# Two more warming matmuls, half as many idle matmuls and another written-out order in a fused attention and mixer kernel

## The chip, the core and the metric

The kernel runs on one core of a Trainium2 chip. The metric is device time in microseconds (us), the median of several executions; lower is better. One further execution was taken with the hardware profiler, and its page and trace are what the prediction reads.

A core has five engines that run their own instruction queues in order: TensorE (PE in the profile; its weight loads stand apart as PEld), VectorE (DVE), ScalarE (ACT), GpSimd (POOL) and SyncE (SP). In this kernel POOL issues the loads, SP issues the stores and the transposing transfers, and PE does every product.

## The reference

For 8 batches, 12 heads, 448 positions and a head width of 64:

```python
scores = scale * np.matmul(q, k.transpose(0, 1, 3, 2))
attn = np.maximum(scores, 0.0) ** 2 / S
x = np.matmul(attn, v)          # then heads side by side: x is (8, 448, 768)
xt = x.transpose(0, 2, 1)
h = np.maximum(xt @ w_tok1, 0.0) @ w_tok2      # 448 -> 256 -> 448 over positions
u = x + h.transpose(0, 2, 1)
h2 = np.maximum(u @ w_ch1, 0.0) @ w_ch2        # 768 -> 1536 -> 768 over channels
return u + h2
```

There is no softmax: scores are clipped at zero, squared and multiplied with v. Inputs and output are float32; products are made in bfloat16.

## The kernel before

The attention is cut into 24 sessions of four heads, three sessions to a batch. The 448 positions are seven chunks (c = 0 to 6) of 64. The channel mixer works by batches and 128-channel blocks, and for its second product by pairs of 128-row tiles, 14 pairs in all. For the last two batches the first channel product, and for all pairs the second one, is made by a scheme of seven block products instead of eight (names Q and P), with sums and differences made on VectorE.

Nothing is scheduled by a planner at run time or at build time. Every operation has a name, and one long string, `ORDER`, lists the names in the order in which they are issued. An entry is `name:how`. For PE operations `how` gives the PSUM banks (0 to 7) that the operation writes; for evictions, copies and sums it is A or D, the engine (ACT or DVE) that does it. Because each engine's queue is filled in this order, `ORDER` decides the sequence on each engine, and the semaphores that follow from the data decide who waits. The check in `run` is only that each name stands behind what it depends on:

```python
            o = self.ops[name]
            assert name not in done and all((d.name in done for d in o.deps)), name
```

The names, with the lines that the profile shows:

- `ldk`, `ldq`, `ldv` s.half: loads of session s on POOL (L286); `ldf`: the first q, loaded in float32 on SP (L345) and turned to bfloat16 by `cast` (L270 on ACT, L272 on DVE); `wt1`, `wt2`, `wc1`, `wc2`: loads of weights (L297, L304, L312, L321). `ident` makes the unit matrix on POOL (masks.py:199).
- `Ts`: transposes of k and q of session s on PE (L391), 56 matmuls of 64 rows, for session 0 in two halves of 28; `cp`: their copy out of PSUM (L270, L272). From session 12 on the transposes are made by transfers (`xk`, `xq`, on SP, after the copies `ik`, `iq`).
- `Ss.c`: scores, four 64-row matmuls (L432) into two banks; `rs.c.e`: eviction of one bank with the clip at zero (L264 on ACT, L266 on DVE); `qs.c`: the square, always on DVE (L439).
- `Vs.c`: the product with v, four 64-row matmuls (L456), which needs the square `qs.c`; `xe`: its eviction (L466 on ACT, L468 on DVE).
- `X`: transposes of x on PE (L491) for the first eight sessions, in halves of four matmuls for the first three, else eight at once; `xc`: their copy into `x_sb`; later sessions use the transfer `xd` on SP.
- `t1` (L500), eviction `rt`, `t2` (L509), sum `u` (L513): the position mixer; `ub`: transfers of its result into `u_sb` on SP.
- `C1.b.e`: first channel product, six matmuls (L545), eviction `c1e` (L264, L266); `Q` (L617) with `m`, `y`, `n`, `h`, `g`: the same for the last two batches.
- `P` (L710) with `s1` to `s4` (L697) and the adds `a`, `b`, `c`, `f` (L725, L727): second channel product; `ws`: the weight sums that it needs; `st`: stores (L759).
- `fill:bank*n`: n idle matmuls on zeros into a bank (L806). They compute nothing that is used; they keep PE busy.

Operations T, S and V use 64 of the array's 128 rows for one matmul and run several side by side; all others use 128 rows. The prediction calls a change from one to the other a change of grouping.

Ahead of `ORDER` PE gets warming matmuls on zeros (L335), 512 columns each. The loads reuse their buffers in rings (four each for k and q, three for v), and a load stands in POOL's queue until the session that held its buffer has been used.

Of the kernel before, what the change touches and what calls it, by code (L numbers as in the profile page):

```python
# [61 lines left out]
ldf.1 ldk0.1 ldf.0 ldk0.0 ldk1.1 ldq1.0 ldq1.1 ldk1.0 cast1.0:A cast1.1:D ldv0.0 ident cast0.0:D cast0.1:A ldv0.1  # L62
T0.1:0 T0.0:1 ldk2.0 cp0.1:A cp0.0:D ldq2.0 fill:2*13 S0.6:23 ldk2.1 S0.2:45 S0.0:67 r0.6.0:A r0.6.1:D S0.1:10
ldq2.1 r0.2.0:A r0.2.1:D S0.4:23 r0.0.0:A ldk3.0 r0.0.1:D S0.3:45 r0.1.1:A ldv1.1 r0.1.0:D S0.5:67 r0.3.1:A ldv1.0
q0.0:D r0.5.1:A fill:0*4 T1.0:01 r0.5.0:A r0.3.0:D ldk3.1 cp1.1:A cp1.0:D ldq3.1 q0.1:D r0.4.1:A ldq3.0 fill:5*19
S1.4:57 S1.1:64 q0.2:D r0.4.0:A S1.2:01 ldq5.0 r1.1.0:A r1.1.1:D fill:3*3 S1.0:32 wt1.1 r1.2.0:A q0.3:D V0.0:64
r1.2.1:A wt1.0 r1.0.1:D V0.1 r1.0.0:A V0.2 q0.4:D T2.0:01 r1.4.1:A ldv2.0 q0.5:D r1.4.0:A S1.3:23 V0.3 ldv2.1
cp2.1:A cp2.0:D ldk5.1 q1.0:D r1.3.1:A fill:7*15 S2.0:75 wt2 q0.6:D S1.6:01 r1.3.0:A r1.6.1:A q1.1:D ldq4.0 S1.5:32
V0.4 r1.6.0:A q1.2:D V0.5 ldk4.1 r1.5.0:A r1.5.1:D V0.6 r2.0.1:A S2.2:10 r2.0.0:D ldk4.0 xe0.1:A q1.3:D xe0.0:A
ldq4.1 r2.2.0:A q1.4:D fill:3*21 X0.0:3 r2.2.1:A q1.5:D S2.3:25 ldv3.1 V1.0:74 xc0.0:A q1.6:D V1.1 ldk6.1 r2.3.0:A  # L70
V1.2 q2.0:D S2.1:61 r2.3.1:A ldq5.1 X0.1:0 q2.2:D r2.1.0:A V1.3 S2.4:32 r2.1.1:A xc0.1:D V1.4 ldv3.0 T3.0:56 q2.3:D
r2.4.0:A V1.5 r2.4.1:A q2.1:D V1.6 cp3.1:A cp3.0:D t1.0.1:0 ldv4.0 xe1.1:D xe1.0:A ldk5.0 fill:1*5 S3.2:13 q2.4:D
rt0.1:A S3.0:25 V2.0:64 ldv4.1 r3.2.1:A r3.0.1:D V2.1 r3.0.0:A S2.5:70 wc1.1 r3.2.0:D S2.6:35 r2.5.0:A V2.2 r2.5.1:D
r2.6.1:A V2.3 ldq6.0 S3.5:21 q3.0:D r2.6.0:A V2.4 S3.3:70 ldq6.1 r3.5.1:A q2.5:D r3.5.0:A q2.6:D fill:5*11 V2.5
r3.3.1:A S3.1:53 q3.2:D X1.0:1 r3.3.0:A t2.0.1:2 q3.5:D r3.1.1:A t1.0.0:0 r3.1.0:A xc1.0:D V2.6 q3.3:D T4.0:73
rt0.0:A ldv5.0 xe2.1:A q3.1:D cp4.1:A ldk6.0 cp4.0:D fill:1*7 X2.1:1 X1.1:5 ldk7.0 t2.0.0:0 u0.1:D xe2.0:A t1.1.0:4
ldv5.1 xc1.1:A xc2.1:D S4.0:73 u0.0:D rt1.0:A S3.4:62 wc1.0 r4.0.1:A t1.1.1:1 r4.0.0:D r3.4.0:A V3.0:54 r3.4.1:D
S3.6:03 rt1.1:A V3.1 r3.6.1:A S4.4:76 r3.6.0:D V3.2 S4.3:12 r4.4.1:A q3.4:D V3.3 r4.3.1:A X2.0:3 r4.3.0:D S4.6:06
r4.4.0:A V3.4 xc2.0:D t2.1.0:2 r4.6.1:A q3.6:D S4.5:17 r4.6.0:A V3.5 ldk8.1 q4.0:D S4.2:36 r4.5.1:A V3.6 u1.0:D
t1.2.0:0 r4.5.0:A ldv6.0 t2.1.1:7 r4.2.1:A r4.2.0:D wc2.11 t1.2.1:1 rt2.0:A xe3.1:D xe3.0:A S4.1:26 T5.0:30 u1.1:D  # L80
ldq7.1 rt2.1:A r4.1.1:A r4.1.0:D X3.0:4 ldq7.0 cp5.1:A t2.2.1:5 cp5.0:D ldk7.1 t2.2.0:1 xc3.0:A q4.1:D V4.0:76
# [5 lines left out]
ldq8.1 S6.1:76 r6.0.0:A r6.0.1:D V5.5 S6.4:03 r6.1.1:A V5.6 ldq8.0 r6.1.0:D r6.4.0:A C1.0.0a:1 xe5.0:D wc2.12
xe5.1:A X4.0:4 q6.0:D r6.4.1:A X5.0:6 ldv7.1 q6.1:D xc4.0:A t2.3.0:7 xc5.0:D C1.0.2a:0 u3.0:D t1.5.0:2 q6.4:D q6.5:D
t1.4.0:5 rt5.0:A C1.0.0 rt4.0:A C1.0.1a:3 c1e0.0:D C1.0.2 t2.5.0:4 c1e0.2:A C1.0.1 u5.0:D S6.6:67 c1e0.1:A T7.0:25
r6.6.0:D r6.6.1:A S6.2:10 S6.3:43 ldk11.0 cp7.0:D cp7.1:A t2.4.1:6 r6.3.1:D ldv8.0 t2.5.1:7 r6.3.0:A t2.4.0:2 u4.1:D  # L90
ldq9.1 r6.2.0:A C1.0.4:5 u4.0:D r6.2.1:A ldk10.1 u5.1:D ldk10.0 S7.3:34 q6.2:D c1e0.4:A S7.0:61 ldv8.1 V6.0:20
r7.0.1:A q6.3:D C1.1.2:7 ldq9.0 r7.0.0:A q6.6:D r7.3.0:A ldq10.1 r7.3.1:D V6.1 c1e1.2:A S7.4:51 wc2.21 q7.0:D
T8.0:63 r7.4.1:A r7.4.0:D V6.2 S7.1:47 wc2.22 cp8.1:A C1.1.5:1 cp8.0:D ldq10.0 r7.1.1:A r7.1.0:D q7.3:D ldq12.0 V6.3
c1e1.5:A S8.0:56 S7.2:37 q7.1:D ldk11.1 V6.4 r7.2.0:A C1.1.7:4 r7.2.1:D ldk12.1 r8.0.1:A r8.0.0:D C1.1.1:1 q7.2:D
c1e1.7:A q7.4:D q8.0:D V7.0:37 c1e1.1:A V6.5 S8.1:65 ws1.1:D V7.1 V6.6 r8.1.1:A V7.2 r8.1.0:D S7.6:41 xe6.1:A
C1.0.5:5 ws1.0:D xe6.0:A r7.6.1:A r7.6.0:D ub0.0 S8.3:60 q8.1:D c1e0.5:A S7.5:21 C1.1.0:4 r8.3.1:A r7.5.0:D ub0.1
# [105 lines left out]
def kernel(ctx: ExitStack, tc: tile.TileContext, q: bass.AP, k: bass.AP, v: bass.AP, moe_w_tok1: bass.AP, moe_w_tok2: bass.AP, moe_w_ch1: bass.AP, moe_w_ch2: bass.AP, out: bass.AP):  # L202
    nc = tc.nc
    B, H, S, D = q.shape
# [129 lines left out]
    for i in range(9):  # L334
        nc.tensor.matmul(warm_ps, lhsT=warm[:, :128], rhs=warm, start=True, stop=True)  # L335
# [451 lines left out]
    for (s, a), o in ue.items():  # L787
        b, i = divmod(s, GS)
# [48 lines left out]
```

## Time and profile before

| what | value |
|---|---|
| median of 3 runs | 353.52 us (352.86 to 354.24) |
| time of the profiled execution | 354.84 us |
| span from its first to its last instruction | 353.1 us |
| mean granted TensorE clock | 0.997 |
| matmuls in the trace | 3645 |
| of these warming / idle matmuls | 9 / 98 |
| DMA | 48.74 MB, mean 138 GB/s |

How to read the lines that follow. On the page, part 1 gives each engine's busy time, its share of the span and its instructions; part 4 gives the chain of work that ended last, by engine. A row of stretches gives the stretch and its length and then, for PE, PEld, DVE, ACT and POOL, the busy time and in parentheses the number of instructions; then the clock, the share of the DMA engines and GB/s. A row of the timeline gives start, length, engine, line, operation, output and input with shapes, and the number of like instructions merged; in square brackets stands the idle time of the engine before it and what ended it. Instructions on one engine overlap in the pipeline, so the price of one among its like is the distance of starts, not its length. A row of DMA issues ends with size and median time from issue to landing.

### The profile page before, as it was taken

What the parts mean: (1) busy time and instruction counts of PE and PEld (TensorE: products, weight loads), DVE (VectorE), ACT (ScalarE), POOL (GpSimd) and SP (SyncE); (2) the same over time, 40 slices, a digit from 0 to 9 for tenths busy, and PEclk for the clock granted to TensorE, in tenths of its full rate; (3) what the DMA queues carried; (4) which work ended last, traced back from release to release, by engine and by line L of the source; (5) the groups of instructions that cost most, each with busy time, mean ns of one, the idle gap of its engine ahead of it and who ended that gap; (6) DMA issues with size and microseconds to landing.
All of it is one profiled execution on the core that took longest, in us unless ns stands there. A gap on an engine that the chain in (4) does not pass through costs nothing.

```text
span 353.1 us, 9074 instructions
## 1 busy us (share of the span) xinstructions
PE 345.2 (98%) x3645; PEld 193.3 (55%) x3645; DVE 304.3 (86%) x581; ACT 215.9 (61%) x443; POOL 92.4 (26%) x157
## 2 busy tenths in 40 slices
PE   7999999999999999999999999999999999999994
PEld 4666556545556555556545565554555565555662
DVE  2799998899988998967699899998989987878973
ACT  3899987888936579874298617778746601452000
POOL 8866515630624523226201602040200000000000
PEclk9999999999999999999999999999999999999998
DMA  8999999799898989999959996779794523730346
GB/s 156 159 173 145 201 190 147 99 183 123 105 193 158 170 147 219 172 162 149 171 111 171 164 167 95 120 124 161 146 110 93 132 44 66 168 65 0 77 115 168
DMA packets 93434, 48.74 MB, mean 138 GB/s; under 512 B 65808, under 2 KB 90064, under 8 KB 93392
## 3 DMA queue, kind: packets, MB, share of 16 engines
q0 software_dynamic: 25904, 21.47, 43.7%
q1 hardware_dynamic: 67168, 26.30, 42.0%
q8 instruction: 28, 0.46, 0.6%
q10 hardware_dynamic: 320, 0.39, 0.4%
q14 instruction: 14, 0.11, 0.1%
HBM read 43.38 MB, written 11.01 MB: 154 GB/s over the span
## 4 chain that ended last, share of the span: by engine, by line
PE 93%; DVE 3%; POOL 1%; issue 1%; ACT 1%; POOLq 0%
PE m_ps L710 27%; PE m_ps L545 24%; PE sc_ps L432 10%; PE acc_ps L456 9%; PE m_ps L617 7%; PE t_ps L500 6%; PE h_ps L509 5%; DVE sq L439 2%; PE kqT_ps L391 2%; PE x_ps L491 1%; PE fill_ps L806 1%; POOL kq_raw L286 1%; ACT sq L264 0%; DVE sq L266 0%; DVE kqT L272 0%
## 5 line engine op out<-in xcount | busy, mean ns | idle before, releaser
L264 ACT ACTIVATE sq<-sc_ps 128x448 bf16<-128x448 f32 x225 | 108.2, 568 | 20.1 <-PE sc_ps L432 19.6
L439 DVE TENSOR_TENSOR sq<-sq 128x896 bf16<-128x896 bf16 x168 | 97.1, 617 | 0.3
L545 PE MATMUL m_ps<-uT_sb,wc 128*128 128x448 bf16 x432 | 90.5, 353 | 0.0
L266 DVE TENSOR_SCALAR sq<-sc_ps 128x448 bf16<-128x448 f32 x111 | 65.2, 618 | 13.3 <-PE sc_ps L432 12.8
L264 ACT ACTIVATE r_sb<-m_ps 128x448 bf16<-128x448 f32 (+3 forms) x93 | 40.1, 464 | 39.5 <-PE m_ps L545 38.0
L545 PEld LDWEIGHTS <-wc 128*128 128x128 bf16 x432 | 40.0, 98 | 42.5 <-issue 8.1
L432 PE MATMUL sc_ps<-kqT 64*64 64x448 bf16 x672 | 57.7, 364 | 0.5
L286 POOL DMA_DIRECT2D v_raw<-in_v_dram x48 | 29.4, 621 | 106.8 <-PE acc_ps L456 68.9
L456 PE MATMUL acc_ps<-sq,v_raw 64*64 64x448 bf16 x672 | 55.1, 354 | 0.0
L710 PEld LDWEIGHTS <-r_sb 128*128 128x128 bf16 x336 | 32.2, 98 | 23.2 <-issue 2.5
L725 DVE TENSOR_TENSOR out_sb<-m_ps,u_sb 128x384 f32<-128x384 f32 x56 | 31.0, 553 | 9.7 <-PE m_ps L710 9.6
L286 POOL DMA_DIRECT2D kq_raw<-in_q_dram x46 | 28.9, 639 | 31.5 <-PE acc_ps L456 16.0
L286 POOL DMA_DIRECT2D kq_raw<-in_k_dram x48 | 29.9, 635 | 24.0 <-PE kqT_ps L391 15.2
L710 PEld LDWEIGHTS <-sums 128*128 128x128 bf16 x252 | 24.4, 98 | 17.6 <-issue 0.7
L513 DVE TENSOR_TENSOR uT_sb<-h_ps,xT 128x448 bf16<-128x448 f32 x48 | 29.1, 618 | 4.7 <-PE h_ps L509 4.6
L432 PEld LDWEIGHTS <-kqT 64*64 64x64 bf16 x672 | 22.8, 107 | 18.0 <-issue 9.7
L710 PE MATMUL m_ps<-wc_t,r_sb 128*128 128x384 bf16 x168 | 31.4, 326 | 0.0
L710 PE MATMUL m_ps<-wc,r_sb 128*128 128x384 bf16 x168 | 31.3, 326 | 0.0
L710 PE MATMUL m_ps<-wc_t,sums 128*128 128x384 bf16 x168 | 30.4, 326 | 0.0
L456 PEld LDWEIGHTS <-v_raw 64*64 64x64 bf16 x672 | 20.6, 106 | 16.5 <-issue 9.9
L264 ACT ACTIVATE r_sb<-t_ps 128x512 bf16<-128x512 f32 (+1 forms) x26 | 14.8, 567 | 23.6 <-PE t_ps L500 23.4
L727 DVE TENSOR_TENSOR out_sb<-m_ps,out_sb 128x384 f32<-128x384 f32 x42 | 22.9, 554 | 4.1 <-PE m_ps L710 3.6
(65 smaller groups left out, 345.3 us busy)
## 6 DMA issues: line engine op xcount, KB each, us to landing
out_dram<-out_sb SPq DMA_DIRECT2D x52, 192.0 KB, 3.0
kq_raw<-in_k_dram POOLq DMA_DIRECT2D x48, 112.0 KB, 4.5
v_raw<-in_v_dram POOLq DMA_DIRECT2D x48, 112.0 KB, 5.0
kq_raw<-in_q_dram POOLq DMA_DIRECT2D x46, 112.0 KB, 4.9
wc<-in_moe_w_ch_dram POOLq DMA_DIRECT2D x2, 1152.0 KB, 11.6
wc<-in_moe_w_ch_dram POOLq DMA_DIRECT2D x3, 576.0 KB, 10.7
u_sb<-uT_sb SPq DMA_TRANSPOSE x54, 3.5
sums<-in_moe_w_ch_dram POOLq DMA_DIRECT2D x1, 576.0 KB, 9.1
```

The lines of the kernel that those rows point to most:

```text
L264: nc.scalar.activation(out, ps, AF.Relu)
L266: nc.vector.tensor_scalar(out=out, in0=ps, scalar1=0.0, scalar2=None, op0=ALU.max)
L286: nc.gpsimd.dma_start(out=raws[t][s % NR[t]][64 * half:64 * (half + 1)], in_=src[b, h0:h0 + 2].rearrange('e (p c) d -> p e (c d)', c=KC))
L432: nc.tensor.matmul(o.ps[e][64 * half:64 * (half + 1), :S], lhsT=lhsT, rhs=rhs, start=True, stop=True, skip_group_check=True)
L439: sq_ops[s, c] = [add(Op(f'q{s}.{c}', 'DVE', lambda o: nc.vector.tensor_tensor(out=buf, in0=buf, in1=buf, op=ALU.mult), ev))]
L456: nc.tensor.matmul(o.ps[half][64 * e:64 * (e + 1), :S], lhsT=r[rows, e, c * D:(c + 1) * D], rhs=sq[rows, e, :], start=c == 0, stop=c == KC ...
L513: nc.vector.tensor_tensor(out=uTs[bb % 2][:, 2 * i + a, off:off + S].rearrange('n (c p) -> n c p', c=KC), in0=t2.ps[:, :S].rearrange('n (p ...
L545: nc.tensor.matmul(ps[:, :S], lhsT=wc1[:, g, e * 128:(e + 1) * 128], rhs=uT[:, g, off:off + S], start=g == 0, stop=g == CC - 1)
L617: nc.tensor.matmul(banks[into][:, :S], lhsT=lhs[:, g, k * 128:(k + 1) * 128], rhs=rhs[:, g], start=after is None and g == 0, stop=g == GH ...
L710: nc.tensor.matmul(banks[into][:, :HN], lhsT=lhs[:, e], rhs=wc2[w][:, e], start=after is None and e == 0, stop=e == EH - 1, skip_group_che ...
L725: nc.vector.tensor_tensor(out=out_[:, cols].rearrange('n (g d) -> n g d', d=128), in0=banks[into][:, :HN].rearrange('n (g d) -> n g d', d= ...
L727: nc.vector.tensor_tensor(out=out_[:, cols], in0=banks[into][:, :HN], in1=out_[:, cols], op=ALU.add)
```

## The change

The diff has two parts. The first adds two warming matmuls:

```diff
-    for i in range(9):
+    for i in range(11):
         nc.tensor.matmul(warm_ps, lhsT=warm[:, :128], rhs=warm, start=True, stop=True)
```

The second replaces the whole string `ORDER`. It holds the same 1,946 operations; the entries `fill` go from nine (13, 4, 19, 3, 15, 21, 5, 11, 7: 98 idle matmuls) to six (7, 4, 19, 3, 12, 4: 49). Its first lines:

```diff
-ldf.1 ldk0.1 ldf.0 ldk0.0 ldk1.1 ldq1.0 ldq1.1 ldk1.0 cast1.0:A cast1.1:D ldv0.0 ident cast0.0:D cast0.1:A ldv0.1
-T0.1:0 T0.0:1 ldk2.0 cp0.1:A cp0.0:D ldq2.0 fill:2*13 S0.6:23 ldk2.1 S0.2:45 S0.0:67 r0.6.0:A r0.6.1:D S0.1:10
+ldf.1 ldk0.1 ldf.0 ldk0.0 ldk1.1 ldq1.0 cast1.0:A cast1.1:D ldk1.0 ldq1.1 ident cast0.0:A cast0.1:D ldv0.0 T0.1:0
+ldv0.1 T0.0:1 cp0.1:A ldk2.0 cp0.0:D ldq2.1 fill:2*7 S0.0:23 S0.5:45 S0.4:67 ldq2.0 r0.0.0:A r0.0.1:D S0.2:01
...
```

Between the two orders the sequence of all engines differs, and so do banks and, for some evictions, the engine: 419 entries on ACT and 575 on DVE become 420 and 574. The loads have another sequence on POOL (`ldv0.0` now behind `ident`; of the weights of the second channel product, `wc2.11` is now last instead of first). Around the points that the prediction names, the orders read:

```diff
-xc3.0:A q4.1:D V4.0:76 S5.0:20 u2.0:D V4.1
...
+V3.2 q3.4:D S4.4:43 xc1.0:A ldk6.0 V3.3 u0.1:D S4.0:16 r4.4.0:A V3.4
```

From P6.13 on, the products and adds of the last two pairs, and the last three stores, stand in the same sequence in both.

More of the change, by code (lines that the diff above doesn't have):

```diff
@@ L77 @@
[L77 to L81, printed above, removed]
@@ L87 @@
[L87 to L91, printed above, removed]
@@ L92 @@
[L92 to L96, printed above, removed]
@@ new lines @@
+r5.6.1:A V5.2 S6.4:41 ldv7.1 xe4.1:D xe4.0:A V5.3 S6.5:03 r6.4.0:A q5.6:D ldk8.1 V5.4 S6.6:65 r6.5.1:A V5.5 r6.5.0:D
+ldv7.0 X4.0:4 r6.6.0:A r6.6.1:D t2.3.1:3 ldq10.1 r6.4.1:A C1.0.2a:0 xc4.0:D u3.1:D C1.0.0a:6 q6.4:D V5.6 q6.5:D
+S6.0:51 S6.1:43 ldv8.0 xe5.0:A xe5.1:D C1.0.0 r6.0.0:A ldk9.0 C1.0.2 r6.0.1:D c1e0.0:A t1.4.0:7 ldq10.0 q6.6:D
+c1e0.2:A r6.1.1:A ldk10.0 r6.1.0:D X5.0:2 rt4.0:A C1.0.3:5 q6.0:D ldq9.1 xc5.0:A q6.1:D ldv8.1 C1.0.1a:1 ldk9.1
+c1e0.3:A wc2.22 t2.4.0:6 t1.5.0:0 u4.0:D wc2.12 t2.4.1:3 rt5.0:A wc2.21 S6.3:47 u4.1:D T7.0:25 r6.3.1:A r6.3.0:D
@@ new lines @@
+ldk10.1 S6.2:60 cp7.1:A C1.0.4:3 cp7.0:D r6.2.1:A r6.2.0:D t2.5.1:7 q6.3:D c1e0.4:A C1.0.5:4 u5.1:D q6.2:D t2.5.0:2
+c1e0.5:A C1.0.1 u5.0:D V6.0:50 c1e0.1:A S7.1:63 S7.0:74 V6.1 r7.1.0:D r7.1.1:A T8.0:21 r7.0.1:A r7.0.0:D V6.2
+cp8.1:A C1.1.7:3 cp8.0:D q7.0:D C1.1.3:6 q7.1:D c1e1.7:A V6.3 c1e1.3:A S7.2:47 V6.4 r7.2.0:A r7.2.1:D S7.6:21 V6.5
+V7.0:36 r7.6.1:A r7.6.0:D V6.6 S8.2:47 V7.1 ldv9.0 xe6.0:A xe6.1:D C1.0.8:1 r8.2.1:A q7.2:D wc2.11 r8.2.0:A q7.6:D
+ldk11.1 S7.3:25 c1e0.8:A q8.2:D S7.4:07 X6.0:4 r7.3.0:A r7.3.1:D C1.1.1:1 r7.4.1:A r7.4.0:D xc6.0:A ub0.0 q7.3:D
@@ new lines @@
+V12.5 r13.4.1:D V13.1 r13.5.0:A S13.6:12 V12.6 q13.3:D ik16:A C1.2.11:7 xq15 ldv15.0 xe12.0:D xe12.1:A ldk17.1
+q13.4:D r13.6.0:A t1.11.0:0 r13.6.1:D xk16 c1e2.11:A q13.5:D iq16:A t2.10.1:5 C1.2.7:4 rt11.0:D xq16 q13.6:D
+t2.11.1:1 u10.1:D c1e2.7:A C1.2.1:2 u11.1:D st5.0 st5.1 V13.2 c1e2.1:A S14.5:70 st3.0 V13.3 S14.2:54 r14.5.0:A
+r14.5.1:D V13.4 xd12 S14.0:12 r14.2.1:A r14.2.0:D V13.5 S14.6:70 r14.0.1:A V13.6 s1.4:D S14.3:45 r14.6.1:A ldv16.1
+ub3.1 s1.3:D P2.3:2 r14.3.1:A s2.4:D ldq19.0 r14.3.0:A s3.4:D P2.4:0 xe13.0:A s2.3:D xe13.1:A s3.3:D r14.0.0:A
@@ new lines @@
+S22.4:06 r21.6.1:A V21.5 r21.6.0:D P1.7:4 r22.4.0:A q22.1:D r22.4.1:A C1.4.11:1 q21.6:D a.7:D st12.1 q22.3:D
+t2.18.0:7 c1e4.11:A ub5.4 t2.18.1:5 q22.4:D t1.19.0:0 u18.0:D s1.7:D C1.5.7:6 rt19.0:A u18.1:D s2.7:D S23.0:17
+c1e5.7:A s3.7:D V21.6 S22.6:05 r23.0.1:A s4.7:D P6.7 xe21.0:A xe21.1:D r23.0.0:A r22.6.0:D C1.5.6:6 xd21 r22.6.1:A
+b.7:D q23.0:D S22.2:73 c1e5.6:A S23.2:21 q22.6:D S23.1:05 r22.2.1:A P7.7 r22.2.0:D r23.2.1:A r23.2.0:D r23.1.0:A
+t2.19.0:6 c.7:D r23.1.1:A P5.7:3 u19.0:D q22.2:D t2.19.1:7 P4.7 f22.7:D u19.1:D P2.7:1 q23.1:D f21.7:D C1.5.0:2
@@ L198 @@
+st25.1 P5.13:2 c.13:D P4.13 f22.13:D st27.1.384 P2.12:1 f21.13:D st25.0 P3.12 st27.0.384 f11.12:D st27.1.0 P3.13
+st27.0.0 f12.12:D st24.1 f12.13:D st24.0 st26.1.384 st26.0.384
 """
```

231 lines of the change are left out of this document (112 added, 119 removed).

## The prediction, made before the changed kernel had run

> **What bounds the kernel now.** I read the page's busy times and chain first, then the stretches between the last idle matmuls and the end, then the start instruction by instruction.
>
> ```profile
> PE 345.2 (98%) x3645; PEld 193.3 (55%) x3645; DVE 304.3 (86%) x581; ACT 215.9 (61%) x443; POOL 92.4 (26%) x157
> ...
> PE 93%; DVE 3%; POOL 1%; issue 1%; ACT 1%; POOLq 0%
> ```
>
> ```profile
> 9.48:13.02 3.54, 3.53 (x32) 2.12 (x32) 2.88 (x6) 2.86 (x7) 3.37 (x6) 1.00 1.10 142
> 13.02:34.10 21.08, 20.36 (x495) 14.03 (x496) 20.62 (x40) 20.77 (x46) 13.69 (x23) 1.00 1.12 161
> 34.10:43.67 9.57, 9.57 (x183) 5.90 (x182) 9.48 (x19) 9.51 (x22) 6.01 (x10) 1.00 1.19 196
> 43.67:348.40 304.73, 304.73 (x2859) 167.15 (x2858) 268.69 (x510) 179.37 (x368) 60.95 (x102) 1.00 0.84 134
> ```
>
> The columns are busy times of PE, PEld, DVE, ACT, POOL. From 43.67 us on PE never idles, so there only PE's amount of work counts. From 13.02 to 34.10 DVE (20.62 of 21.08) and ACT (20.77) are full too, and PE's share is padded with idle matmuls: there evictions and squares set the pace. So three things set the end: when the evictors start, how much of their work stands ahead of the point at which PE takes over, and PE's work behind it.
>
> **The start.** Timeline rows: start, length, engine, line.
>
> ```profile
> 1.19 4.02 PE L335 MATMUL warm_ps<-out_sb 128*128 128x512 bf16 x9 [1.19 <-DVE out_sb L332]
> ...
> 4.29 0.66 POOL L286 DMA_DIRECT2D kq_raw<-in_k_dram  x1
> 4.87 0.67 POOL L286 DMA_DIRECT2D v_raw<-in_v_dram  x1
> ...
> 5.81 0.58 ACT L270 ACTIVATE kq_raw<-side 64x448 bf16<-64x448 f32 x1 [1.08 <-DMA side<-in_q_dram]
> ...
> 5.82 0.53 POOL masks.py:199 TENSOR_SCALAR_AFFINE_SELECT ident<-ident 128x128 bf16<-128x128 bf16 x1
> ...
> 6.40 1.52 PE L391 MATMUL kqT_ps<-ident,kq_raw 64*64 64x64 bf16 x56 [1.19 <-POOL ident masks.py:199]
> ...
> 7.86 1.57 PE L806 MATMUL fill_ps<-out_sb 128*128 128x128 bf16 x13
> 7.96 0.62 DVE L272 COPY kqT<-kqT_ps 128x896 bf16<-128x896 bf16 x1 [1.77 <-PE kqT_ps L391]
> ...
> 9.48 2.99 PE L432 MATMUL sc_ps<-kqT 64*64 64x448 bf16 x28
> ...
> 13.07 0.64 PE L391 MATMUL kqT_ps<-ident,kq_raw 64*64 64x64 bf16 x56
> ...
> 13.64 1.24 PE L806 MATMUL fill_ps<-out_sb 128*128 128x128 bf16 x19
> 13.76 0.62 DVE L272 COPY kqT<-kqT_ps 128x896 bf16<-128x896 bf16 x1 [0.33 <-PE kqT_ps L391]
> ```
>
> The first transposes wait for ident. The first 56 take 1.46 us (6.40 to 7.86), the next 0.57 (13.07 to 13.64): PE runs at half clock until about 13.0, though the clock column shows 1.00 there, so I take the clock from the durations. Thirteen idle matmuls therefore cost 1.62 us (7.86 to 9.48), about 0.107 each and 0.23 around them, while the copy that the first scores need ends at 8.58: 0.9 us of pure delay.
>
> After the change one POOL load fewer (0.58 = 4.87 - 4.29) stands ahead of ident, so it ends at 5.77 instead of 6.35. Nine warming matmuls take 4.02 us, 0.43 each and some 0.2 of drain; two more move their end from 5.21 to 6.06, drain included. So the first transposes start at about 5.95, without a gap, 0.45 earlier; the second half's cast ends at 6.39, in time. Seven idle matmuls at half clock take 7 x 0.107 + 0.23 = 0.98. First scores: 5.95 + 1.46 + 0.98 = 8.39, 1.09 earlier; the copy (8.13) is done. If the clock rises at 13.0 as before, session 1's transposes now fall into the slow stretch: seven scores of 0.37 (28 matmuls take 2.99, drain included) and four idle matmuls end at 11.5, the transposes take 1.28 to 1.46 instead of 0.57, and the copy starts at about 12.85 instead of 13.76: 0.9 earlier. I take **1.0 us** of earlier evictions; bounds 0.5 (the slow transposes starve ACT and DVE more) and 2.1 (early clock, below).
>
> **Amount of work.** Both orders hold the same products, evictions and DMAs; only idle matmuls (98 to 49), warming matmuls (9 to 11), sequence, banks and the engine of some evictions change. Row groupings (64-row T, S, V against 128-row others) alternate less often: 67 + 66 changes become 59 + 58.
>
> ```profile
> 67.58 0.36 PE L456 MATMUL acc_ps<-sq,v_raw 64*64 64x448 bf16 x4
> 67.87 1.31 PE L545 MATMUL m_ps<-uT_sb,wc 128*128 128x448 bf16 x6
> 69.11 0.38 PE L456 MATMUL acc_ps<-sq,v_raw 64*64 64x448 bf16 x4
> 69.32 0.36 PE L432 MATMUL sc_ps<-kqT 64*64 64x448 bf16 x4
> 69.51 0.68 PE L391 MATMUL kqT_ps<-ident,kq_raw 64*64 64x64 bf16 x56
> ```
>
> ```profile
> 298.90 19.86 PE m_ps L617 x105
> ```
>
> Undisturbed, a 448-column matmul comes every 0.189 (19.86 / 105), six in 1.135; between two 64-row groups six take 1.24 (67.87 to 69.11). A V ahead of them takes 0.29 instead of the 0.19 of 69.32 to 69.51, the V behind 0.21. A round trip thus costs 0.10 + 0.105 + 0.02 = 0.23, a change 0.115.
>
> Now the take-over point. For each product that waits for DVE or ACT I add that engine's work, in order, up to what it waits for, to PE's work from there to the end; the largest sum binds. DVE's and PE's prices:
>
> ```profile
> 20.93 1.15 DVE L266 TENSOR_SCALAR sq<-sc_ps 128x448 bf16<-128x448 f32 x2
> 21.99 3.29 DVE L439 TENSOR_TENSOR sq<-sq 128x896 bf16<-128x896 bf16 x6
> 25.20 0.42 DVE L272 COPY x_sb<-x_ps 128x512 bf16<-128x512 bf16 x1
> 25.54 1.15 DVE L439 TENSOR_TENSOR sq<-sq 128x896 bf16<-128x896 bf16 x2
> ...
> 23.69 2.86 ACT L264 ACTIVATE sq<-sc_ps 128x448 bf16<-128x448 f32 x6
> 26.25 1.12 ACT L270 ACTIVATE kqT<-kqT_ps 128x896 bf16<-128x896 bf16 x1
> ```
>
> ```profile
> 34.10 0.61 PE L491 MATMUL x_ps<-ident,xT 128*128 128x128 bf16 x8
> 34.54 0.54 PE L509 MATMUL h_ps<-wt,r_sb 128*128 128x448 bf16 x2
> 34.92 0.61 PE L500 MATMUL t_ps<-x_sb,wt 128*128 128x128 bf16 x8
> ...
> 44.07 0.36 PE L456 MATMUL acc_ps<-sq,v_raw 64*64 64x448 bf16 x4
> ```
>
> By starts, a score eviction on DVE is 0.53 (1.06 for two), a square 0.535 (3.21 for six), an x_sb copy 0.34, an eviction on ACT 0.427 (2.56 for six); a kqT copy lasts 0.62 like a score eviction (row 13.76), so I count it alike, as xT evictions and u; two X take 0.44, a t2 0.38, a first-sessions t1 about 0.45.
> - Before, V4.1 binds: 60 steps of 0.533 and 4 x_sb copies on DVE, 33.3 us. The row 44.07 tests it: PE's end at 348.4 lies 304.3 behind, of which 1.6 I find as waits (single products longer than their like), the rest work.
> - After, V3.4 binds: 46 such steps, 2 copies and one rt (0.35, between a copy and 0.53), 25.6 us: 7.8 less.
> - PE ahead of V4.1 before, but behind V3.4 after: 6 S and 4 V (10 x 0.19), one T (0.44), two small X (0.44), one double (0.45), three t1 (1.34), five t2 (1.89): 6.5 us more PE work to come.
> - Changes of grouping behind it: 101 become 95, 6 x 0.115 = 0.7 less.
>
> Sum: -7.8 + 6.5 - 0.7 = **-2.0 us**; the largest sum over ACT falls too, from 336.0 (t1.3.0, behind 33.6 us of ACT work) to 333.6 (S4.1, behind 27.4), so ACT doesn't take DVE's place. The 49 idle matmuls (0.054 each at full clock, 2.6 us) are not counted again: the evictors cover them, and PE now waits where they ran. Were that cover gone, they would be worth 2.6.
>
> What I cost at nothing: queues and the tail.
>
> ```profile
> wc<-in_moe_w_ch_dram POOLq DMA_DIRECT2D x3, 576.0 KB, 10.7
> ...
> kqT<-side SPq DMA_TRANSPOSE x24, 3.4
> ...
> x_sb<-xT SPq DMA_TRANSPOSE x16, 4.9
> ```
>
> ```profile
> 348.44 0.56 DVE L727 TENSOR_TENSOR out_sb<-m_ps,out_sb 128x384 f32<-128x384 f32 x1 [0.42 <-PE m_ps L710]
> 349.02 0.47 ACTq L759 DMA_DIRECT2D out_dram<-out_sb  x1
> ```
>
> In PE work the shortest lead of a kqT transpose over its scores is 8.4 us after (7.75 before), of an x_sb transpose 9.0 (9.8), of the weight load wc2.11, now the last of its kind, 14 over the sums made from it: all above the landing times. Without that cover a late transpose stalls PE and, behind it on SP, the u_sb transposes, by 1 to 3 us. The last products, adds and three stores have the same sequence.
>
> Total -2.0 - 1.0 = **-3.0 us**. The profiled execution (span 353.1, time 354.84, so 1.7 around it) becomes 350.1 and 351.8; against the median of 353.52, 1.3 below that execution, it is **350.5**.
>
> **Rivals.**
> - *The clock rises early.* Before, PE idles 1.19 us ahead of the first transposes; after, it doesn't from 1.19 on. If that lifts the clock by 6.2, the transposes end at 6.7 (cast at 6.39), the copy at 7.4, and scores start 2.1 earlier, at full clock: -2.0 - 2.1, 349.4. For it: full clock came at 13.0 only after an almost unbroken stretch (3.53 busy of 3.54). Against: 4.02 us of warming alone didn't lift it. The Trainium skill (TensorE: Matmul & The Clock Gate, Part 1: The HAM clock gate) says that a free-running window of some 3.4 us, busy throughout, lifts the clock; by that rule two windows from 1.19 on, 8.0 us, suffice at the latest. The trace agrees that 5.2 us with a gap did not suffice. Chance 0.22.
> - *The later part gives it back.* PE waits 1.6 us in all behind V4.1; with fewer changes, longer runs of scores meet DVE (88% busy: 268.69 of 304.73). If these waits more than double, to 3.5, 1.9 of the 3.0 goes: 352.4. Against: from session 6 on the take-over sums lie 2.4 us and more under the largest in both orders. Chance 0.22.
> - *The clock falls back* (slower). With half the idle matmuls PE has 14.7 us of products and 2.0 of idle matmuls for some 21.7 from session 1 to S4.0, busy 0.77, against 0.97 before (20.36 of 21.08). If the gate counts that as idle, each 3.4 us at half clock makes its 2.3 us of useful work 4.6: +1.2. It decides from three such windows: 350.5 + 3.6 = 354.1; four or five give 355.3 to 356.5. Nothing in the trace tests it: its clock never fell before the end. By the same page a fall needs an idle window, and no such one arises, which would exclude this. Chance 0.07.
> - *The gap isn't closed*: ident and warming end within 0.3 us of each other, so it costs 0.2 at most and is in the bounds.
>
> **The numbers.** Forecast 350.5 has 0.49, the rivals 0.22, 0.22, 0.07. The range goes from below the early clock (348.9, with 0.5 off) to above the half-returned gain (352.8). About 0.5% (1.77 us) can be told from no change: faster means below 351.75: nearly all of forecast and early clock (0.45 + 0.21) and a quarter of the second rival, 0.72; slower, above 355.29, a part of the clock's fall and stray stalls, 0.06; the rest 0.22.
>
> **What would show it.** First transposes at 5.9 to 6.0, no idle time ahead of them; first scores at 8.4 (7.4 with an early clock); the second copy of kqT by 12.9; V3.4 near 35.4, and PE without idle time from there; the span's end 3 us earlier. Wrong if the clock row shows halves after 13 us, if single products stand longer than their like by over 3 us in all behind V3.4, or if DVE idles before 30 us.

## The result and the profile after

| | before | after |
|---|---|---|
| median, side by side | 353.84 us (8 executions, 352.75 to 354.79) | 351.36 us (8 executions, 350.78 to 352.56) |
| profiled execution / span | 354.84 / 353.1 us | 351.28 / 349.5 us |
| matmuls in the trace | 3645 | 3598 |

The ratio is 0.9938, with a 95% interval of 0.9917 to 0.9958: about 2.2 us faster. It is a ratio of means. By the medians it is 2.5, by the two profiled executions 3.6; the profiled execution of before stands above all eight of its others, so the ratio is what counts.

Busy times and the chain of waits of the page after:

```profile
PE 340.4 (97%) x3598; PEld 190.9 (55%) x3598; DVE 303.4 (87%) x581; ACT 216.5 (62%) x443; POOL 92.2 (26%) x157
...
PE 93%; ACT 4%; DVE 1%; issue 1%; ACTq 0%; DVEq 0%
```

The chain still is PE's. The stretches after (PE, PEld, DVE, ACT, POOL, then clock, DMA share, GB/s):

```profile
7.96:10.93 2.97, 2.84 (x33) 1.45 (x33) 2.51 (x5) 2.54 (x6) 2.97 (x6) 1.00 1.11 158
10.93:26.62 15.69, 13.23 (x338) 8.38 (x338) 15.62 (x31) 15.58 (x35) 12.61 (x21) 1.00 1.11 159
26.62:33.91 7.29, 7.17 (x158) 4.63 (x161) 7.29 (x15) 7.27 (x18) 2.94 (x6) 1.00 1.13 182
...
43.67:344.86 301.19, 301.19 (x2836) 167.30 (x2828) 265.57 (x505) 178.97 (x366) 61.02 (x101) 1.00 0.86 135
```

From 10.93 to 33.91 DVE is busy for 22.91 of 22.98 and ACT for 22.85: the two evictors set the pace up to V3.4, and PE, with fewer idle matmuls, has holes (13.23 of 15.69) that cost nothing in themselves. From V3.4 on PE has no gap longer than 0.3.

Which of the two evictors is the last has changed. In the chain of waits of before, DVE's squares have 21% of the time from 9 to 44 us and ACT's evictions of scores 4%; after, from 7 to 34.5 us, it is 8% and 38%. The last link ahead of PE's own work, as the chain shows it, is ACT too, and the product behind V3.4 waits for it:

```profile
33.75 0.25 ACT x_sb L270
34.00 0.45 ACT sq L264
34.56 0.61 PE x_ps L491 x8
```

The start instruction by instruction:

```profile
1.19 4.88 PE L335 MATMUL warm_ps<-out_sb 128*128 128x512 bf16 x11 [1.19 <-DVE out_sb L332]
...
6.00 1.24 PE L391 MATMUL kqT_ps<-ident,kq_raw 64*64 64x64 bf16 x56
...
7.17 0.56 PE L806 MATMUL fill_ps<-out_sb 128*128 128x128 bf16 x7
7.28 0.62 DVE L272 COPY kqT<-kqT_ps 128x896 bf16<-128x896 bf16 x1 [0.78 <-PE kqT_ps L391]
7.96 2.58 PE L432 MATMUL sc_ps<-kqT 64*64 64x448 bf16 x28 [0.23 <-DVE kqT L272]
...
10.93 0.64 PE L391 MATMUL kqT_ps<-ident,kq_raw 64*64 64x64 bf16 x56
11.62 0.62 DVE L272 COPY kqT<-kqT_ps 128x896 bf16<-128x896 bf16 x1
```

The transposes start without idle time ahead. Their second half and everything behind it run at full clock: the seven idle matmuls last 0.56 where at half clock they would last 0.93 (the thirteen of before, 1.57, less 6 x 0.107), and the 28 score matmuls take 2.58 where they took 2.99. The clock rose at about 6.7 us here, not at 13.0.

### The profile page after: what moved, and what is told of

Same layout as the page of the kernel before. It is cut to its first block, busy times and chain, and to the rows that moved or that the text cites. A ratio compares the mean times of both kernels' runs of the same rounds, so it can differ in the third digit from the quotient of the medians.

```text
span 349.5 us, 8983 instructions
## 1 busy us (share of the span) xinstructions
PE 340.4 (97%) x3598; PEld 190.9 (55%) x3598; DVE 303.4 (87%) x581; ACT 216.5 (62%) x443; POOL 92.2 (26%) x157
## 4 chain that ended last, share of the span: by engine, by line
PE 93%; ACT 4%; DVE 1%; issue 1%; ACTq 0%; DVEq 0%
PE m_ps L710 28%; PE m_ps L545 24%; PE sc_ps L432 9%; PE acc_ps L456 9%; PE m_ps L617 7%; PE t_ps L500 6%; PE h_ps L509 5%; ACT sq L264 3%; PE warm_ps L335 1%; PE kqT_ps L391 1%; PE x_ps L491 1%; DVE sq L439 1%; ACT xT L466 0%; DVE sq L266 0%; ACT kqT L270 0%
## 5 line engine op out<-in xcount | busy, mean ns | idle before, releaser
L266 DVE TENSOR_SCALAR sq<-sc_ps 128x448 bf16<-128x448 f32 x114 | 66.8, 616 | 12.3 <-PE sc_ps L432 12.2
L264 ACT ACTIVATE r_sb<-m_ps 128x448 bf16<-128x448 f32 (+2 forms) x96 | 42.0, 464 | 45.0 <-PE m_ps L545 43.2
L432 PE MATMUL sc_ps<-kqT 64*64 64x448 bf16 x672 | 59.2, 354 | 0.6 <-DVE kqT L272 0.2
L456 PE MATMUL acc_ps<-sq,v_raw 64*64 64x448 bf16 x672 | 56.3, 354 | 0.3
L432 PEld LDWEIGHTS <-kqT 64*64 64x64 bf16 x672 | 24.3, 105 | 18.4 <-issue 9.6
L710 PE MATMUL m_ps<-wc,r_sb 128*128 128x384 bf16 x168 | 30.6, 326 | 0.0
L500 PE MATMUL t_ps<-x_sb,wt 128*128 128x256 bf16 (+1 forms) x216 | 25.0, 261 | 0.0
```

The costliest lines, as they stand in the source:

```text
L264: nc.scalar.activation(out, ps, AF.Relu)
L266: nc.vector.tensor_scalar(out=out, in0=ps, scalar1=0.0, scalar2=None, op0=ALU.max)
L432: nc.tensor.matmul(o.ps[e][64 * half:64 * (half + 1), :S], lhsT=lhsT, rhs=rhs, start=True, stop=True, skip_group_check=True)
L456: nc.tensor.matmul(o.ps[half][64 * e:64 * (e + 1), :S], lhsT=r[rows, e, c * D:(c + 1) * D], rhs=sq[rows, e, :], start=c == 0, stop=c == KC ...
L500: nc.tensor.matmul(o.ps[:, j, :], lhsT=wt1[:, c, j * 128:(j + 1) * 128], rhs=x_sb[:, p0:p1, c, :], start=c == 0, stop=c == 3)
L710: nc.tensor.matmul(banks[into][:, :HN], lhsT=lhs[:, e], rhs=wc2[w][:, e], start=after is None and e == 0, stop=e == EH - 1, skip_group_che ...
```

## The experiments

"Expected" is quoted as it stood before each run. Ratios are to the kernel before, run alongside; its own median was 353.5 to 354.3 from one experiment to the next, so the medians of two experiments can be compared to some tenths of a us only. Each execution also has a mean granted clock: one period at half rate (3.41 us in the records) lowers it by 0.5 x 3.41 / 350 = 0.005, so 0.997 to 1.000 means no such period after the first rise, and 0.995 or less one or more. How late the first rise came doesn't show in it.

**The start alone, put on the order of before.** Eleven warming matmuls, `ident` ahead of `ldv0.0`, seven idle matmuls instead of thirteen:

```diff
-cast1.1:D ldv0.0 ident
+cast1.1:D ident ldv0.0
-fill:2*13 S0.6:23
+fill:2*7 S0.6:23
-    for i in range(9):
+    for i in range(11):
```

> The order of before with the new start alone: eleven warming matmuls, ident ahead of ldv0.0 on POOL, 7 instead of 13 idle matmuls ahead of the first scores. Theory (the evictors' earlier start is worth 1.0 us with a late clock, 2.1 with an early one, and adds to the sequence's own gain): 1.0 to 2.1 us under before (351.7 to 352.8), first transposes at 5.9 to 6.0 and first scores at 7.4 to 8.4 in the profile. Rival 'all of the gain is the start': 2.2 us or more under before. Rival 'the start is hidden, PE's sequence is all': within 0.4 us of before.

Measured: 352.90 us (352.55 to 354.58), ratio 0.9982 (0.9969 to 0.9996): 0.6 to 0.9 us, a little less than the 1.0 to 2.1 expected. First transposes and first scores stand where they were expected, at 5.90 and 8.22:

```profile
5.90 1.60 PE L391 MATMUL kqT_ps<-ident,kq_raw 64*64 64x64 bf16 x56
7.43 0.56 PE L806 MATMUL fill_ps<-out_sb 128*128 128x128 bf16 x7
8.22 2.58 PE L432 MATMUL sc_ps<-kqT 64*64 64x448 bf16 x28 [0.22 <-DVE kqT L272]
```

**Only the two warming matmuls**, on the order of before:

> The kernel before with eleven warming matmuls alone. Theory 'the start's gain is the clock rising at 5 to 8 us instead of 10 to 13': the clock rises before 8.1 us, thirteen idle matmuls then take 0.9 instead of 1.6, and the time is 0.5 to 1.2 us under before (352.6 to 353.3) with a narrow spread. Rival 'the start's gain is ident and fewer idle matmuls': within 0.3 us of before.

Measured: 352.94 us (352.75 to 353.41), ratio 0.9976 (0.9962 to 0.9990).

```profile
6.18 0.63 PE L391 MATMUL kqT_ps<-ident,kq_raw 64*64 64x64 bf16 x28 [0.31 <-POOL ident masks.py:199]
...
7.75 0.90 PE L806 MATMUL fill_ps<-out_sb 128*128 128x128 bf16 x13
8.71 2.58 PE L432 MATMUL sc_ps<-kqT 64*64 64x448 bf16 x28
```

This is the time that was expected if the gain is the clock (352.6 to 353.3). Thirteen idle matmuls, and scores half a microsecond later than in the kernel above, yet the same time. In both the scores run at full clock; on top of the two warming matmuls the earlier `ident` and the six idle matmuls add nothing that could be measured. What the two matmuls do shows in the single executions. The 23 of before that were run beside this kernel fall into three groups: nine at 352.74 to 353.49 with a mean clock of 0.997 or more; seven at 353.55 to 353.95 with 0.995 or less; seven at 354.17 to 354.99, six of them with 0.997 again, as the profiled execution of before has (354.84), whose clock rose only at 13.0. All twelve with eleven warming matmuls stand where the first group stands. The lowest time is the same (352.74 and 352.75): the two matmuls don't make the best execution faster, they take the two slower groups away (nearly: one of the twelve of the kernel above, 354.58, has a mean clock of 0.992).

**`ident` and the idle matmuls without the two warming ones** (9 of them), on the order of before:

> The kernel before with ident ahead of ldv0.0 and seven idle matmuls, but nine warming matmuls. The recorded reasoning (with a late clock the earlier start is worth 1.0 us): 1.0 us under before (352.7). Theory 'the start's gain is the clock': 0 to 0.6 us under before (353.1 to 353.8), spread as wide as before's.

Measured: 353.14 us (352.35 to 354.60), ratio 0.9992 (0.9974 to 1.0010): no difference that can be told, where the prediction's reasoning wanted 1.0 us. In its profile the clock rose early all the same (28 scores in 2.58 from 7.69), but its times spread up to 354.60, where all but one of the twelve with eleven warming matmuls and the same start lie under 353.3. Its five fastest, 352.35 to 352.53, lie below every execution of before: when the clock rises early, the earlier scores (7.69) are worth some 0.3.

**The changed kernel with nine warming matmuls:**

> The changed kernel with nine warming matmuls, ident and seven idle matmuls as changed. Theory 'unbroken warming lifts the clock before 8 us, and that is the start's gain': PE stands idle 0.5 to 0.7 us ahead of the first transposes, the clock rises behind 9 us in most runs, and the time is 0.6 to 1.4 us over the changed kernel (352.0 to 352.8) with a wider spread. Rival 'the gain is ident and fewer idle matmuls': within 0.3 us of the changed kernel.

Measured: 352.16 us (351.41 to 354.25), ratio 0.9975 (0.9953 to 0.9996): 0.8 above the changed kernel, as expected. But its profile (351.44) doesn't show the late rise that was expected: PE idles 0.37 ahead of the first transposes, and the clock is up at 6.10. What the record shows is falls. Nine of its twelve executions have a mean clock of 0.995 or less, its five slowest (353.44 to 354.25) among them, and of the changed kernel's eight one. So the two warming matmuls, 0.86 us of PE, come with fewer periods at half clock and a lower time; by which step they prevent the falls is not shown.

**The changed order with the old start** (`ldv0.0` ahead of `ident`, thirteen idle matmuls, nine warming):

> The new order with the old start: nine warming matmuls, ldv0.0 ahead of ident, 13 idle matmuls ahead of the first scores. Theory: the sequence's own gain stays, 1.0 to 2.0 us under before (351.8 to 352.8), first scores at 9.4 to 9.5. Rival 'the start is all': within 0.4 us of before. Rival 'the sequence is all': 2.2 us or more under before.

Measured: 352.79 us (351.35 to 357.93), ratio 0.9969 (0.9951 to 0.9987). So the order alone is worth 1.0 to 1.1 us, at the lower edge of what was expected. The profile fell on the longest execution, 357.93; it is of use for what the clock does. Stretches of one record each:

```profile
16.46:19.88 3.42, 3.08 (x103) 1.96 (x106) 3.34 (x7) 3.42 (x8) 2.35 (x4) 1.00 1.14 155
19.88:23.29 3.41, 1.64 (x28) 0.76 (x20) 3.41 (x7) 3.41 (x9) 2.59 (x5) 1.00 1.00 135
23.29:26.70 3.41, 3.41 (x65) 1.76 (x68) 2.74 (x7) 3.29 (x8) 2.54 (x4) 0.50 1.10 147
```

PE is busy for 1.64 of 3.41 us, and the next period runs at half clock. A second fall, 197.37 to 200.79, follows a wait of 2.7 us ahead of S18.1. The Trainium skill (TensorE: Matmul & The Clock Gate, Part 1: The HAM clock gate) has the clock fall after an idle window of about 3.4 us; the period fits, but here a half-busy window was enough. So the fall that the prediction held to be excluded by that rule does happen. Busy time alone doesn't decide it, though: in the kernel with three V turned round, further down, a stretch with less work was followed by full clock:

```profile
190.22:193.64 3.42, 1.45 (x29) 0.66 (x28) 1.69 (x3) 1.96 (x4) 0.00 (x0) 1.00 1.53 152
193.64:197.05 3.41, 2.95 (x30) 1.70 (x34) 2.40 (x5) 2.49 (x6) 2.08 (x4) 1.00 1.23 267
```

What else decides stays open.

**No idle matmuls behind the first scores**, in the order of before (85 removed) and in the changed one (42 removed). Of each the diff shows one place, before first:

```diff
-q0.0:D r0.5.1:A fill:0*4 T1.0:01
+q0.0:D r0.5.1:A T1.0:01
...
-V0.4 S1.1:45 cp2.0:A q1.0:D ldk4.1 q1.2:D r1.1.0:A ldq4.0 fill:2*12 S2.1:23
+V0.4 S1.1:45 cp2.0:A q1.0:D ldk4.1 q1.2:D r1.1.0:A ldq4.0 S2.1:23
```

> The order of before without the 85 idle matmuls behind the first scores. Theory (evictions and squares set the pace up to V4.1, idle matmuls are covered): within 0.6 us of before, and PE shows idle time where they stood, up to 34 us. Rival 'PE's own work is the sum everywhere': 85 x 0.054 = 4.6 us under before. Rival 'the clock falls back without them': 1.2 us over before for each 3.4 us at half clock, and the clock row shows it behind 13 us.

> The changed kernel without the 42 idle matmuls behind the first scores. Theory: within 0.6 us of the changed kernel (350.8 to 352.0), clock at full from its rise on. Rival 'PE's work is the sum': 42 x 0.054 = 2.3 us under the changed kernel. Rival 'the clock falls back': 1.2 us or more over it, and with the first rise later than 7 us in the profile, because scores alone keep PE less busy.

Measured: 353.10 us (352.27 to 353.80), ratio 0.9982 (0.9967 to 0.9997), and 353.10 us (351.80 to 355.81), ratio 0.9988 (0.9966 to 1.0010). At full clock 85 idle matmuls are 4.6 us of PE; taking them out gave 0.6 (by the interval 0.1 to 1.2), so the evictors do cover most or all of them. Its profile (353.62) has a first rise at 10.25 and no fall, and lies 1.3 above its fastest executions: a second case in which a late rise goes with a slow execution.

In the changed kernel taking them out loses 1.7, against the expectation of none. Five of its twelve executions have a mean clock of 0.995 or less, as the rival of a falling clock has it. But there is more in it. By the spans the loss is 1.2 (medians 350.8 and 349.6), and the rest lies outside the span, where this kernel alone has up to 2.9 us instead of 1.8, from a cause that isn't known. And in its profiled execution (354.57) a late load of k opened a gap. The clock, up at 4.64, was at half from 8.05 to 11.47:

```profile
7.78 1.02 PE L391 MATMUL kqT_ps<-ident,kq_raw 64*64 64x64 bf16 x28 [1.58 <-DMA kq_raw<-in_k_dram]
8.73 0.93 PE L806 MATMUL fill_ps<-out_sb 128*128 128x128 bf16 x7
9.72 1.71 PE L432 MATMUL sc_ps<-kqT 64*64 64x448 bf16 x16
```

**The one long wait of PE in the early part filled** with thirty idle matmuls. The changed kernel's waits, from 7 to 45 us, and the stretch around them:

```profile
PE x_ps L491 <- ACT xT L466: 1.7, 1, 1.7
```

```profile
16.94:20.35 3.41, 2.10 (x31) 1.00 (x28) 3.41 (x8) 3.41 (x9) 2.65 (x5) 1.00 1.08 144
```

The same wait can be followed by half clock, as the clock's periods lie on it. In the kernel with idle matmuls in dense runs, below, the same wait ends at the same time (X0.0 at 20.96 in both), but the periods lie 0.95 us later:

```profile
17.89:21.30 3.41, 1.64 (x28) 0.76 (x20) 3.41 (x7) 3.41 (x9) 2.98 (x6) 1.00 1.10 147
21.30:24.72 3.42, 3.42 (x69) 1.77 (x72) 2.75 (x7) 3.30 (x8) 3.42 (x6) 0.50 1.23 181
```

The filling:

```diff
-q1.5:D ldk5.0 X0.0:2
+q1.5:D ldk5.0 fill:2*30 X0.0:2
```

> The changed kernel with 30 idle matmuls (1.6 us) put into PE's wait of 1.9 us ahead of X0.0. Theory 'the wait is covered by the evictors, but a 3.4 us stretch with PE half busy can make the clock fall': no run is lost to a fall there, so the spread narrows and the median is 0 to 0.5 us under the changed kernel (350.9 to 351.4); no half clock between 13 and 40 us in the profile. Rival 'idle matmuls cost PE time': 1.6 us over it. Rival 'the clock's falls have no part in it': exactly as the changed kernel, same spread.

Measured: 351.56 us (351.28 to 351.94), ratio 0.9938 (0.9916 to 0.9961). The median is the changed kernel's, so nothing is won by filling it, and thirty idle matmuls in an evictor's wait cost nothing. All six executions have a mean clock of 0.997 or more. Six are too few to call the narrower spread shown. Of the profiles of this order without the filling and with the 42 idle matmuls, three of five show a period at half clock behind this wait; of the three with it, none.

**The price of a change of grouping**: one idle matmul, put eleven times between two 64-row products, and eleven times between two 128-row products of the changed kernel. In both kernels all idle matmuls, the 49 too, work on the unit matrix instead of zeros:

```diff
-V11.0:17 c1e2.0:A S11.6:23
+V11.0:17 c1e2.0:A fill:2*1 S11.6:23
```

```diff
-q11.5:D c1e2.6:A P2.1:0
+q11.5:D c1e2.6:A fill:0*1 P2.1:0
```

> The changed kernel with eleven single idle matmuls, each between two 64-row products behind 100 us of PE work: eleven more round trips between groupings. Idle matmuls use the unit matrix as operands here. Theory (0.23 for a round trip, 0.055 for the matmul): 3.1 us over the changed kernel (354.2 to 354.8). Rival 'a change of grouping is hidden': 0.6 us over it.

> The control to the one before: the same eleven idle matmuls, each between two 128-row products, no change of grouping added. Theory: 11 x 0.055 = 0.6 us over the changed kernel (351.8 to 352.3), so that the difference between the two is 2.5 us. Rival 'the idle matmul itself is dear': as slow as with the round trips.

Measured: 356.33 us (355.54 to 358.11), ratio 1.0080 (1.0051 to 1.0108), and 353.45 us (352.86 to 354.16), ratio 0.9994 (0.9976 to 1.0011): 5.0 and 2.1 over the changed kernel, where 3.1 and 0.6 were expected. The first of these fences is from the kernel with the idle matmuls among scores, the second from the other:

```profile
132.80 0.38 PE L456 MATMUL acc_ps<-sq,v_raw 64*64 64x448 bf16 x4
133.11 0.23 PE L806 MATMUL fill_ps<-ident 128*128 128x128 bf16 x1
133.40 0.38 PE L432 MATMUL sc_ps<-kqT 64*64 64x448 bf16 x4
```

```profile
201.03 0.22 PE L806 MATMUL fill_ps<-ident 128*128 128x128 bf16 x1
201.30 1.14 PE L710 MATMUL m_ps<-wc,r_sb 128*128 128x384 bf16 x6
```

The medians differ by 2.9 us, 0.26 a round trip against the 0.23 of the prediction. But the control isn't clean. Of the eleven lone idle matmuls in dense runs seven take 0.275 from start to start (as 201.03 to 201.30) and four 0.055, as among their like; what sets the seven apart is not known. Among scores nine take 0.285 and two 0.16, and the product ahead takes 0.10 more than the 0.21 usual behind a 128-row product. By all these slots the two places differ by 0.17. A period at half clock in the early part is in both profiles; a wait of 1.4 us at S12.5 is in the first alone. The price in this isolated form stays open between 0.17 and 0.26.

**Three V ahead of the last S of their runs.** Behind the take-over the changed kernel's waits stand at the ends of runs of 64-row products:

```profile
126.51 0.51 PE L432 MATMUL sc_ps<-kqT 64*64 64x448 bf16 x4
126.70 0.51 PE L456 MATMUL acc_ps<-sq,v_raw 64*64 64x448 bf16 x4
126.89 0.67 PE L432 MATMUL sc_ps<-kqT 64*64 64x448 bf16 x4
127.19 0.56 PE L456 MATMUL acc_ps<-sq,v_raw 64*64 64x448 bf16 x4
127.68 1.12 PE L545 MATMUL m_ps<-uT_sb,wc 128*128 128x448 bf16 x5
```

```profile
125.44 1.69 DVE L266 TENSOR_SCALAR sq<-sc_ps 128x448 bf16<-128x448 f32 x3 [0.39 <-PE sc_ps L432]
```

The starts are 0.19 apart up to 126.89; S11.2 then holds PE for 0.30 and V10.6 for 0.49, where 0.19 and 0.29 (V before a 128-row product) are undisturbed. One of S11.2's two banks is still being evicted by DVE until about 127.1. Turned round, V10.6 runs while that bank comes free (likewise V12.6 and S13.6, V14.6 and S15.1); the thirty idle matmuls are kept:

```diff
-S11.2:50 r11.5.1:A V10.6
+V10.6 S11.2:50 r11.5.1:A
```

> The changed kernel with the filled wait, and with V10.6, V12.6 and V14.6 put ahead of S11.2, S13.6 and S15.1, whose second bank is still being evicted when they start. Theory 'the waits behind V3.4 are scores that meet evictions still running': the three waits of 0.26 to 0.31 us shrink to 0.1, 0.5 us under the filled-wait kernel (350.9 to 351.2). Rival 'the wait only moves to the next product': as the filled-wait kernel.

Measured: 350.98 us (350.20 to 357.04), ratio 0.9941 (0.9916 to 0.9966). The three places shrank: the pair V10.6 and S11.2 has 0.15 of wait instead of 0.31, V14.6 and S15.1 0.12 instead of 0.26, and S13.6 0.05, where with V12.6 it had 0.28. The median is as expected, 0.6 under the kernel with the filled wait. Seven of twelve executions lie at 350.2 to 351.0, below nearly all of the changed kernel's, but five stand at 351.9 to 357.0 (the next expectation counts eight and four), and the profile fell on one of these (352.90):

```profile
PE sc_ps L432 <- DMA kqT<-side: 2.4, 1, 2.4
```

Its transfer to S18.1 was issued late; SP's queue and the landing times between 164 and 196 us:

```profile
182.24 1.49 SPq L479 DMA_TRANSPOSE x_sb<-xT  x1
183.83 3.25 SPq L414 DMA_TRANSPOSE kqT<-side  x2
```

```profile
kqT<-side SPq DMA_TRANSPOSE x6, 8.3
```

In the kernel with the filled wait alone the same two transfers were issued at 180.10, and the median landing time in that stretch was 6.7.

**Those two transfers earlier in SP's queue**, right behind S15.6, the last reader of their buffer, and ahead of a u_sb and an x_sb transfer:

```diff
-S15.1:02 r15.3.0:A ub3.4 q15.2:D
+S15.1:02 r15.3.0:A q15.2:D
...
-S15.6:26 S16.0:15 c1e3.0:A S16.1:73 q15.4:D xq18
+S15.6:26 xq18 xk18 ub3.4 xd14 S16.0:15 c1e3.0:A S16.1:73 q15.4:D
```

> The kernel with the three V ahead of the last S of their runs, with the two transposing transfers of session 18 issued right behind S15.6 (the last reader of their buffer) and ahead of a u_sb and an x_sb transfer, instead of behind them. In the profile of the version without this, S18.1 waits 2.43 us (2.6 with the slot) for the transfer, which was issued near 187 and landed near 194, and four of its twelve times stand at 351.9 to 357.0 while the other eight stand at 350.2 to 351.0. Theory: the transfer stands too late in SP's queue; issued about 4 us earlier it lands before S18.1 even when the DMA engines are slow, so the wait at S18.1 is under 0.3 us, the profiled span is 348.5 to 349.0 and the median 350.6 to 350.9 with the highest below 352.5. Rival: the DMA engines themselves are full there (busy 9 of 10 in nearly all slices from 164 to 186), so another transfer is late in its place (u_sb or x_sb, 1 us or more on PE between 180 and 200), and a quarter or more of the times stay above 351.9.

Measured: 350.90 us (350.25 to 354.27), ratio 0.9920 (0.9895 to 0.9946), profiled span 348.7. No wait is left at S18.1, and no other transfer took its place:

```profile
178.98 2.56 SPq L413 DMA_TRANSPOSE kqT<-side  x2
181.59 1.27 SPq L524 DMA_TRANSPOSE u_sb<-uT_sb  x1
```

```profile
126.35 0.70 PE L455 MATMUL acc_ps<-sq,v_raw 64*64 64x448 bf16 x8
126.73 0.51 PE L431 MATMUL sc_ps<-kqT 64*64 64x448 bf16 x4
127.18 1.12 PE L544 MATMUL m_ps<-uT_sb,wc 128*128 128x448 bf16 x5
```

One of ten executions stands above 351.8 instead of five of twelve. That one (354.27, mean clock 0.990, two periods at half clock) shows that the expectation of no execution above 352.5 was too much. Its median is 0.46 below the changed kernel's; the intervals of the two ratios overlap, so it is the fastest version seen, but not shown to be faster than the changed kernel.

## Why the prediction was right, and where it was not

The time, 351.36, lies 0.9 above the forecast of 350.5 and inside the range; the direction was right. Step by step, against the profile after:

| step | forecast | early clock | measured |
|---|---|---|---|
| first transposes | 5.95, no gap | 5.95 | 6.00, no gap |
| first scores | 8.39 | 7.4 | 7.96 |
| second copy of kqT | 12.85 | | 11.62 |
| V3.4 | 35.4 | | 33.91 |
| from V3.4 to PE's end | 310.1 | | 310.95 |

- *What bounds* held in the main: evictors full up to V3.4, PE behind it. That ACT doesn't take DVE's place did not hold. By the chain ACT is the last of the two for most of that stretch, and the product behind V3.4 comes 0.35 late because it waits for ACT.
- *The start* was wrong in its mechanism. The forecast kept the clock's rise at 13.0 and took its 1.0 us from `ident` and six idle matmuls. The rise came at 6.7, the first rival (0.5 later than the 6.2 it assumed, hence first scores at 7.96 and not 7.4). The two warming matmuls alone give 0.9976, the whole start 0.9982, `ident` with fewer idle matmuls 0.9992. In size the step came out near its 1.0, by luck: on the order of before 0.6 to 0.9 us (ratio, medians), and in the changed order 1.1 to 1.4 for the whole start (352.79 to 351.36) and 0.8 to 1.3 for the two matmuls (352.16 to 351.36). The first rival's 2.1 us hold against the one profiled execution, whose late rise is that of a third of the executions of before; against the median of before they are too much, since most of its executions don't start that late. Only one execution of each kernel is profiled; that the other late ones rose late too is argued from their times and mean clocks, and from one more profile (rise at 10.25, 353.62).
- *The amount of work* held in its sum and failed in one term. The stretch from the take-over point to PE's end, in the kernel with the order of before and the new start, and then in the changed kernel:

```profile
42.19:346.50 304.31, 304.31 (x2854) 166.82 (x2849) 268.18 (x509) 178.88 (x368) 61.39 (x103) 1.00 0.84 134
```

```profile
33.91:344.86 310.95, 310.67 (x3000) 173.46 (x2995) 275.20 (x524) 187.78 (x385) 66.89 (x111) 1.00 0.87 137
```

  The forecast's undisturbed products are 304.3 - 1.6 = 302.7 in the first and 302.7 + 6.5 - 0.7 = 308.5 in the second. So **the waits behind the take-over, put at 1.6 in both, are 1.6 and 2.5: +0.9. Of the work this is the mis-sized term.** Counted by place, against slots of 0.19, and 0.29 ahead of a 128-row product, the waits I find are 0.9 and 2.1, so the term lies between +0.9 and +1.2. V3.4 lies 8.3 behind its 25.6 us of DVE work, V4.1 8.9 behind its 33.3 (42.19): -0.6, for which no cause is shown. With the -2.0 of the sum that makes -1.7, and the profiled spans of the two kernels go from 351.2 to 349.5, -1.7. By medians the order's part is 1.5 (352.90 to 351.36), with the old start 1.0 (353.77 to 352.79). The second rival named the mechanism, runs of scores meeting DVE, and overstated it (3.5); 2.1 of the 2.5 stand in eleven places, all at ends of runs of 64-row products. Turning three pairs round takes 0.5 of it back; that the stretch is 310.17 in the last kernel, 0.8 less, is in part the 0.35 behind V3.4, which is gone with the filled wait already.
- *The price of a change of grouping* doesn't disagree with the kernel as a whole: with it the products behind V3.4 add up to the measured time but for 0.4 of waits that have no place. But six changes are 0.5 to 0.8 by the range of the test, so the whole can't settle it; taken alone it stayed between 0.17 and 0.26.
- *Idle matmuls at nothing* was right as far as the evictors go: 85 of them, 4.6 us of PE, cost some 0.6, thirty more none. It left out that they can be worth something: without the 42 the changed order is 1.7 slower.
- *The clock falls back* was held to be all but excluded, and does occur, in the kernel before more often than after: eight of the 23 executions above have a mean clock of 0.995 or less, one of the changed kernel's eight. The middle group of seven lies 1.0 us above the first group (medians 353.76 and 352.76, for one period each by most of the mean clocks), where the forecast took 1.2 a period; in the changed kernel that one execution (351.70) is 0.3 above the median.
- *Queues at nothing* was right for the typical execution. The lead of a kqT transpose, 8.4 us at the shortest, is no safe cover where its landing alone takes 8.3 in a busy stretch: in one profile of this order and in one of it with three pairs turned, S18.1 waited 2.7 and 2.4.

So in the profiled execution the span is not longer than forecast but 0.6 shorter (349.5 against 350.1): V3.4 came 1.5 earlier, mostly by the early clock (the second copy of kqT came 1.2 earlier), and the waits behind it cost 0.9 more. The median lies 0.9 above the forecast for another reason. The forecast took 1.3 off, the distance of before's profiled execution from its median, and that distance went with the late clock: the changed kernel's profiled execution (351.28) stands at its median. That these errors leave only 0.9 is in part luck.

## What to carry to other kernels

A start is costed with more than one execution: where the clock rises at a varying moment, one profile shows one throw, and the groups in the times and their mean clocks show the others. Before idle matmuls are counted as work, ask whether an evictor sets the pace there; if so they are nearly free, and what matters is whether PE is left half empty for some 3.4 us, which in five profiled stretches here was followed by half clock and in others was not. Before an engine is called the one that binds, look at the chain after the change: with two evictors equally full the other one can become the last. When a sequence gets fewer changes of grouping, recount the waits at the ends of the longer runs: here the last score of a run met a bank that was still being evicted, and an independent product put ahead of it took over half of that wait away.

## What the hardware did that was not expected

- The clock column gives 1.00 from the first instruction, though up to its first rise (6.7 us after, 13.0 before) every matmul takes twice its time (idle matmuls 0.107 instead of 0.054); the rise shows in durations only.
- One record's length of half work brought the next period to half clock (1.64 of 3.41 us busy, in three kernels); 2.10, in the changed kernel, did not, where the same wait lay otherwise on the periods. Elsewhere 1.45 did not either.
- A lone 128-column matmul with weights of its own in a dense run took 0.275 us in seven places, five times its 0.055 among its like, and 0.055 in four.
- With the DMA engines loaded, the median landing time of the same transposing transfers in the same stretch was 6.7 us in one execution (filled wait) and 8.3 in another (three V turned round), whose orders differ there by little; issued 3.7 us later as well, one came late enough to stop PE for 2.4.
